# A new order table for a planned attention and gated MLP kernel

## The chip, the core and the metric

The kernel is one program on one core of a Trainium2 chip. What is measured is the time of one execution on the device, in microseconds (us); lower is better. A core has five engines that run their own instruction streams in order: TensorE (PE), VectorE (DVE), ScalarE (ACT), GpSimd (POOL) and SyncE (SP), which here issues nearly all DMA transfers.

## What is computed

```python
scores = (1/sqrt(64)) * q @ k.T                     # 8 batches, 8 heads, 576 positions, head dim 64
cum    = cumsum(log(clip(f, 1e-4, 1)), axis=-1)
scores = where(causal, -1e9, scores + cum[..., :, None] - cum[..., None, :])
attn   = softmax(scores, axis=-1)
x      = (attn @ v), the heads side by side         # 8 x 576 x 512
gate   = sigmoid(causal depthwise conv of x, 5 taps, conv_w)
out    = (gate * (x @ w_val)) @ w_out
```

All is float32 in and out, and the result must keep float32 precision. For that most products are made of two parts: a value is split into a rounded part that PE takes in one pass (type fp32r) and the rest, and three products of parts are added up.

## The kernel before

The work is a list of some three thousand steps. `tile_decay_attention_gated_mlp` first adds every step to a `Plan`, each with the engines that may do it, what it reads and writes, and the PSUM banks that it takes. Then `Plan.order` unpacks the string `ORDER`: a word for each step, which says which step comes next and on which engine it runs, and behind these a word for each set of PSUM banks, which says where it lies. The instructions are issued in that order, and dependencies are added so that each engine and the DMA queue keep it. So the table alone decides three things: the order on every engine, the engine of a step that several may do (`any_`), and the bank of each product (`home`).

```python
        steps, homes = words[:len(self.nodes)], words[len(self.nodes):]
        ...
            self.home[k] = list(range(h, h + self.width[k]))
        for w in steps:
            yield self.nodes[w >> 3]["fn"], codes[w & 7]
```

The heads are taken in 32 pairs, four to a batch. For pair i, buffer i % 2 of most tiles is used (names with two numbers in the trace, one for even and one for odd pairs):

- `load_pair` and `load_rest` load q and k as `Xr` (608 KB) and v as `vt` (576 KB). From the fifth pair on `plan_t` splits `Xr` into `Xh` (a cast) and `Xl` (a subtraction). `Xl` has one buffer for all pairs.
- `plan_s` makes the scores on PE in four groups, which take 4, 2, 2 and 1 banks of the 8: the first two groups hold the longest rows. To each the decay is added by products with `st` and `pkr` or `pl`. DVE adds the mask and takes the row minimum (line 469, `red`), ACT takes the exponential (line 473, `ex`) and writes `P`; then the banks are free. DVE transposes `P` into `T` (line 510).
- `plan_pt` sends `T` to `U` in eight DMA transfers of 196 KB, the "blocks", and the row sums through DRAM (`zd`, then two `zb`).
- `plan_pv` multiplies `U` with `vt` on PE (54 instructions of the program, PV below), DVE scales the result into `x` (line 559), and `x` is split into `xh` and `xl` (line 571, the subtraction). The gate's convolution runs as products on PE for the first four pairs (`CV`), and later as multiplications (`tm`, lines 282 and 284) and additions (line 602, `gate`), and a tanh.
- `plan_moe`, once a batch, makes `val` on PE (Mv: 16 steps of six matmuls of 288 columns), multiplies it by the gate on DVE (line 632, `h`), splits `h` into `hh` and `hl` (line 646), and makes the output (Mo: two steps of six matmuls of 512 columns for each tile of rows), which goes out through `ot`.
- `plan_cw` and `plan_w` decode the weights `conv_w`, `w_val` and `w_out` into `wall` in the first part of the run. They come in pieces of 512 KB, which land in `ot` or `gate`.

All DMA but one goes through SP's queue (line 289).

Of the kernel before, what the change touches and what calls it, by code (L numbers as in the profile page):

```python
# [40 lines left out]
ORDER = (
    "c-n1J2}qRb|DSp1a88|5=hQiMPMuTd)H!udom1zOG=sE+w1TvPbPLi7(hAZF(hAH9(k)20AYFrW6Vf$EHzBPc-GVfOw1od|wY&A>|GqrW^FH6>^Zk53-&X|+"
    "f?j}lAS(z8GJ^1+_aGPOCMW@tf*|1CARZJ8VuJ2~YQWn-J3u?(e}W!@K7k-G3|I<%3`)S8LH9u|pnC9A5CSHHwuAP<w?jKYcfnmCGI$%j7t{}W0H%UDU<FtN"
    "-UZcyaWD<E8LCX7!2-}0C>v&hUW7)W?NBGw0(OA|;0|aETn$yi`=AZr!-zrX3B)LL2s#a2gw8^{p{vkw=n}LUybs<E-hhf>9pF~50@e*Sz;?j;;Jx5Rm>t#%"
    "KLFFDbi#iIKZ3Qv<H$kyGuRPW7km_c7xn};4z{H9!r#DN!N%d&VGm%=lp**c_&n?bYzf>C_Q0m$w_#Uc3D`9FDLf224x0m$fNii<@EO<!m<a#?3b>A1gs;MP"
    "0!wfp<s)nzPDr_pLZ(ntI4QxDy#N~!rHB9>pa9H3EX4)Xq?}55j0gay5lDD_3Kb5(3Gj=E?v$;-9O43kgjhzf;R}c{Kn&Nw`w=UM%PCAm6EKX}lQIbmAT|&$"
    "Q$`SnQ??*G0W*9ir4D%`r4`);OduTawUmP?4am1Cw^B}|%%?yRF`yM_2R2j2Qb0&QJchWJf<^QKlPP;rX~+RUhwKN~NEFhHJeVp%;*kNQ961MkM7fark*&z%"
    "$X}2TQKLu#x+B$qI)enzJ*gPfxl}6p4bqN6qFIPV6az&@T}z!tNl+h<OQ=Uk4w{deMLk2RQLCuW$S267Xfr~NxQlv)tWEm`m;yS{=aDd!4k18yp+$%XsO!i@"
    "z=>D}wjf^O6zCvg1-OE&MhDPZ^lhXC{T5e?-T<8FC>jN6M%N-Pp&QY=5dCNXatr+eO@M&$%jkP(Je~pBm3A|=71e|Y5ohsGOmi9^@;tRAZ8(*OaiAtrXV4?5"
    "N#b(q7<wvoBb9_%Nu5hoVXzo*+8SDl5kgRD^XMq57Bz_upqQA$skpRilo1ocC?E|e3uF^rgE@-QL7b2isWyx#Z9j^ZCQoyvvD0*ENsK>jH_@C{kEu@kiP(XP"  # L50
    "rFk)DQODBI_|CKd<b2vLOb_a}w0;a7e<f`?O@hPVsv$851E<E-L0I^^X=GdrrUTQAX~*z!dmui1H|BcUgESHTCgvby4OfSk<1b-8r^WCM_%~@fd=>t7ngO?o"
    "Gvgm)Jh*235awChQ;Z7_!?i%}V?LxUV(hqXNEp`+>49`YUZuUpjAQyC?=ZuVLCACbA^a$0jJ%BBz&wJi;3GH}=@=1=og{bT+wnd4etZXh7(amDPkaIy!B60)"
    "@t^RuxEf*;4vjrYtj0Cs>WNoz_lf<)bGQ~94%<z9Po9NL5C@19><jW7v4<$Y0t60rfrugK2{P<3af)~hM<(d77Q!;ojP;Q`gwIqrHbxpwe@Cn$NeE#AjK(0W"
    "LKY!+3G0w$h!1;!peFoD7LhiH=Lvj*oJ1o%Ab?3b2`EwodxXFyeIh3ac+wTZcC3zcoUoTrjopR4PN37a5iBH7`WZqUsTnJ#-6phP8%eTsRQfg20n#xnEgheJ"
    "gyc$Rr|Z&BV*TlZBvJY^k~#e>_A{vu8%uvgdPTa4y-R|Td$9oY4e1H#e)^X5VJwFHfHaYgf{tL%lRl6h5(v<#bS14WolKUHyVD!e+tV53E2N(E=JewvHF=fR"
    "k<O*Hr1Qx;8U5*JNV9|)@)BX1K!@&SXlRRs!Sofv1a><OOq?grrFY;q2p_SF>Ako&>7Z14Mk{RycZ|_U`;gv7JI4sn9%Gwm7Fv`xi2I!Gq&>xQGDdOZI73D?"
    "4VLkdmdHR7HRJ{C@eF&$?>K<|2D>ezlZK?zi3c)fac45BnUahTSOU?Lah7%@1DVPpM#)0r&J1;ih3q72iRUu{<Z#9%#xxC+QAHl5?ag4N4$>OP&oZxM^wP#@"
    "rx+L-IpZo#kV;B@l{rgWqz%z_ke6wF3^GkYl&2a}pE3yaCbEUdOzq2{(e0^DVk?<PZzBikqYQLb7g<VQWQ;RDWezfy7^ldN)B}vsjKPfYjG>Gn#wtTaKf;L7"
    "Ut~;W_)=~3X~sI^H2o6!D%nWCOyAA~m|pq}{f~?b^rehO<`{iC3&FfWZ(<&%&(jCV4$2<-Bt4o6$s#a^$hYVx=p3euqF_>)HS~jY3)4ptGKpCp_C30jsiA0@"
    "HL3OV7-c;p#tgIHXILnXtN^o$QlHw&q-51mkd$`jE($<7&HR<A$l6DtQizlb%s`el>nNp_63wd4I!WPDI9at>&*_($-4tQg1oIZNF-u6f!Gva7vU(_M%zI2;"  # L60
    "W)mBmd5!Wk3(Q!i@5@@D&oDQcX3hq^mc5wuk}1ukGEj`06jJ6qb1>^C_EJ`F7Mo$qe9LUjx<k2|)tRNrWM&R!5g89Dqm-_!H<{kdwyejL1b-sSm?>wBX6<Hw"
    "$eg1rP*$_H@kNX~?2RllL&rGEhO(yFN|vADX81BY*;v*ryO-U?jx$EtSJ^rii8an1WdBJy%yMw57$FvuRh8M08Q}P{W0^Iq6RaqwF7q9wiNDCc#Y(b{Wj19Z"
    "sHa)=td7jy%*(8Mtk>+HGTZnz)&&-hx`%ax1#o`ib2vy&g1yT2vOZFT90KQ2&Oz2Xn?^mw=dq|9fVz#X<FKg;&Q{Ko91-;)zm9X3-<`RKBV{e}FL4GkWz=h#"
    "gZzV>C4Mh|h_9jkk~z)4%J1hK=FIX(`4Q?%&Pe7A=LBad=eNvN{ub&j&RfoU&KPH&^O4Wv-s4PVTBuO&B&UvgpS8x3atYb*b2!=5Y!VmCRb&gZf$Y<qO^!Aj"
    "B0y#{xqGOtY!B6veSs6nK1f|)?c`6f=2#;FgrGXxAevx>skPb5taa92zDCfP%@Mq3;n^}Sm`xA}1$L1|fM!z#0fAG{oK0g#1&6Z_QGd=>2-xgrIVZCHTr*eB"
    "7PDXFxVT5DQIU>2oLwub7R+Sp*|pq<f<CG$C(4}`D8ysg^VzckGkYtylln5-n6q85mOYu>z-{J|a$2}=v+r=BIjw@NqRs41!DDU*mzTrL=@qmI8U;_eU4qlu"
    "*qnCmRl$9(H0N@5lVFj%TQn@VkbPZpliI_b;GU=6$Q~5D5ZsoW<MxS$sAJT9qCwFW>NW1DXh>wrnWT1##zn270q(M(OEfK76L5uXB9U-YP?ZzNu?aO|SI%SV"
    "tmKl^B321wIZkn}s43^N&?|gOt<Cu<CnPiqkL4_J4-0PypNhsMr-e!3DtCceBRnDO$XOJ<kbLCs5nd4X<N)F&5lL7tTor+M1Tj*4PzV)v=TOBs-nxh>d_zU?"
    "ewR>q9uY@8kb@PzlzpIz#6dBK7Z$yiT+0#iC{jSG<h_;M6s}5;Qib%FoOKCDs+AI?Lh0_DksKe-BE2ga5l#s;JiL5Z_&^d9gXIqCgs?_@O1vzb6?ThFylN?0"
# [729 lines left out]
```

## Time and profile before

| what | us |
|---|---|
| median of three executions | 564.57 |
| all three | 564.47, 577.34, 564.57 |
| the profiled execution | 569.91 |
| its span, first to last instruction | 568.2 |
| PE busy / DVE / ACT / POOL | 486.0 / 445.7 / 369.9 / 293.0 |

The profile is of one execution. The span runs from its first to its last instruction. "Busy" is the time in which an engine had an instruction in work; a PE that is busy may still run at the lower of its two clocks, which the column of the granted clock tells (1.00 is 2.4 GHz, 0.50 is 1.2 GHz).

### The profile page before, as it was taken

How to read it: one execution, taken by the hardware profiler on the slowest of the kernel's cores; microseconds unless marked ns; L12 is line 12 of the kernel's file. 1: busy time of each engine (PE TensorE's matmuls, PEld its weight loads, DVE VectorE, ACT ScalarE, POOL GpSimd, SP SyncE). 2: the span in 40 equal slices, each digit the busy share in tenths (PEclk: the TensorE clock that was granted, in tenths of full speed). 3: DMA queues.
4: the chain of work that ended last, by engine and by line, in shares of the span. 5: the costliest groups of instructions: out<-in, count | busy, mean ns of one | idle time of the engine just before them, and what ended most of it. 6: DMA issues, size and time to landing. Idle time of an engine off the chain costs nothing.

```text
span 568.2 us, 15877 instructions
## 1 busy us (share of the span) xinstructions
PE 486.0 (86%) x6096; PEld 419.9 (74%) x6096; DVE 445.7 (78%) x1150; ACT 369.9 (65%) x968; POOL 293.0 (52%) x296
## 2 busy tenths in 40 slices
...
GB/s 267 110 216 244 203 226 181 184 172 146 204 223 204 193 215 237 205 206 247 181 258 222 221 174 269 252 190 239 221 240 194 238 278 167 185 207 179 101 39 92
DMA packets 50268, 114.08 MB, mean 201 GB/s; under 512 B 11664, under 2 KB 28048, under 8 KB 50192
## 3 DMA queue, kind: packets, MB, share of 16 engines
...
## 4 chain that ended last, share of the span: by engine, by line
DMA 27%; PE 25%; DVE 19%; ACT 10%; SPq 8%; issue 6%; POOL 5%; DVEq 0%; POOLq 0%; ACTq 0%
PE banks L262 25%; DMA Xr<-in_x_dram 13%; SPq L289 8%; DMA U<-T 8%; DVE T L510 6%; DVE banks L469 5%; ACT P L473 4%; DMA out_dram<-ot 2%; POOL Xl L390 2%; DMA zb<-zd 1%; ACT Xh L277 1%; DVE x L559 1%; DVE gate L602 1%; DMA cwu<-in_conv_w_dram 1%; ACT tm L282 1%
## 5 line engine op out<-in xcount | busy, mean ns | idle before, releaser
L473 ACT ACTIVATE P<-banks,negm 128x192 f32<-128x192 f32 (+3 forms) x256 | 145.9, 578 | 37.2 <-DVE negm L469 35.9
L469 DVE CUSTOM_DVE_ANT_0 banks<-banks,mk 128x192 f32<-128x192 f32 (+3 forms) x256 | 137.8, 579 | 14.8 <-PE banks L262 9.3
L510 DVE STREAM_TRANSPOSE T<-P 128x640 f32<-128x640 f32 (+3 forms) x128 | 120.3, 962 | 21.6 <-ACT P L473 14.9
L262 PE MATMUL banks<-U,vt 64*64 64x128 f32 (+1 forms) x3456 | 112.2, 271 | 28.6 <-DMA U<-T 18.9
L262 PEld LDWEIGHTS banks<-U,vt 64*64 64x64 f32 x3456 | 106.6, 143 | 38.0 <-issue 20.8
L262 PE MATMUL banks<-xh,wall 128*128 128x288 f32 x512 | 113.5, 305 | 7.5 <-ACT P L473 4.5
L602 POOL TENSOR_TENSOR gate<-gate,tm 128x576 f32<-128x576 f32 x64 | 90.9, 1421 | 33.9 <-DVE gate L602 11.3
L390 POOL TENSOR_TENSOR Xl<-Xr,Xh 128x512 fp32r<-128x512 f32 (+1 forms) x56 | 78.3, 1415 | 47.0 <-PE banks L262 20.9
L262 PEld LDWEIGHTS banks<-xh,wall 128*128 128x128 f32 x512 | 85.6, 191 | 14.2 <-ACT P L473 5.9
L262 PE MATMUL banks<-wall,hh 128*128 128x512 f32 x288 | 93.2, 405 | 2.4 <-ACT x L277 1.2
L282 ACT ACTIVATE tm<-x,cw 128x576 f32<-128x576 f32 x101 | 76.5, 775 | 17.9 <-DVE gate L602 12.1
L262 PE MATMUL banks<-xl,wall 128*128 128x288 f32 x256 | 76.2, 298 | 0.0
L262 PE MATMUL banks<-st,pkr 64*128 64x288 f32 (+3 forms) x320 | 52.1, 363 | 25.7 <-ACT P L473 12.8
L262 PEld LDWEIGHTS banks<-wall,hh 128*128 128x128 f32 x288 | 52.2, 190 | 15.0 <-issue 1.7
L262 PEld LDWEIGHTS banks<-st,pkr 64*128 64x128 f32 x320 | 29.9, 191 | 42.7 <-ACT P L473 15.5
L571 POOL TENSOR_TENSOR xl<-x,xh 128x576 fp32r<-128x576 f32 x28 | 40.5, 1446 | 32.3 <-ACT xh L277 19.2
L262 PE MATMUL banks<-wall,hl 128*128 128x512 f32 x144 | 56.6, 393 | 0.0
L473 ACT ACTIVATION_READ_ACCUMULATOR P<-banks,negm 128x1 f32 x256 | 51.0, 199 | 0.0
L262 PEld LDWEIGHTS banks<-xl,wall 128*128 128x128 f32 x256 | 48.9, 191 | 0.3
L602 DVE TENSOR_TENSOR gate<-gate,tm 128x576 f32<-128x576 f32 x48 | 40.7, 848 | 8.3 <-ACT tm L282 7.5
L277 ACT CAST Xh<-Xr 128x512 fp32r<-128x512 f32 (+1 forms) x38 | 23.5, 644 | 32.5 <-DMA Xr<-in_x_dram 32.4
L559 DVE TENSOR_TENSOR x<-banks,zb 128x256 f32<-128x256 f32 x64 | 24.2, 411 | 25.3 <-ACT x L277 24.6
(106 smaller groups left out, 739.1 us busy)
## 6 DMA issues: line engine op xcount, KB each, us to landing
...
Xr<-in_x_dram SPq DMA_DIRECT2D x32, 608.0 KB, 6.8
...
```

What stands on the lines that cost most here:

```text
L262: nc.tensor.matmul(out, lhsT=lhsT, rhs=rhs, start=start, stop=stop)
L277: (eng.copy if eng is nc.scalar else eng.tensor_copy)(out=out, in_=in_)
L282: eng.activation(out=out, in_=in_, func=AF.Copy, scale=col)
L289: lambda e: (nc.sync if e == "SP" else nc.scalar).dma_start(out=out, in_=in_), reads, writes, **kw)
L390: eng.tensor_tensor(out=Xl[r][:, a - XQ:e - XQ], in0=Xr[r][:, a:e], in1=Xh[r][:, a - XQ:e - XQ].bitcast(F32), op=ALU.subtract)
L469: nc.vector.tensor_tensor_reduce(out=sl, in0=sl, in1=add, op0=ALU.add, op1=ALU.min, scale=-0.125, scalar=3.0e38, accum_out=negm[r][:, col])
L473: nc.scalar.activation(out=dst, in_=bank(key)[:, a0:a0 + ext], func=AF.Exp, bias=negm[r][:, col], scale=-1.0, accum_out=zs[r][:, col])
L510: dve("DT", dt(2 * w), base + 0.35 + 0.03 * n, lambda t=t, w=w: nc.vector.transpose(out=blocks(64 * FB[t], [(32, 2), (64, 2 * t + 3), (CW, ...
L559: nc.vector.tensor_tensor(out=bass.AP(to.tensor, to.offset, [to.ap[0], (P, 4), (32, 2), (1, 32)]), in0=bank(keys[n])[:, 0:L0 // 2].rearran ...
L571: any_("xl", {"POOL": 1.4, "DVE": 0.67}, p, lambda eng: eng.tensor_tensor(out=xl[s], in0=xv, in1=xh[s][:, :].bitcast(F32), op=ALU.subtract ...
L602: any_("cva", {"POOL": 1.4, "DVE": 0.67}, pp, lambda eng, to=to: eng.tensor_tensor(out=gt, in0=gt, in1=to, op=ALU.add), [tk, gk], [gk])
```

## The change

Only the string `ORDER` is another one. It holds as many words as before, and the steps, their buffers and their dependencies are the same. The transfers of the blocks were taken as longer when it was made, and the DMA queue as served first come, first served.

```diff
--- before.py
+++ after.py
@@ -39,70 +39,70 @@
 ORDER = (
-    "c-n1J2}qRb|DSp1a88|5=hQiMPMuTd)H!udom1zOG=sE+w1TvPbPLi7(hAZF(hAH9(k)20AYFrW6Vf$EHzBPc-GVfOw1od|wY&A>|GqrW^FH6>^Zk53-&X|+"
...
+    "c-nnZc}SFN`<{7caaNsGXVqDCR-IL6)me2`omFR*^cbWiq!py6Agv&+Agv&+Ag#cxApHu`Q;;5m^dzLmApH{33er=MW{{TfJEyF3zVpZLeR!Ycdair9?)xEu"
...
```

Of the 402 sets of banks 224 lie elsewhere. Of the 32 second score groups, three (of the 4th, 12th and 13th pair) took a bank with no other step of PE between them and the last one that wrote it; now none does. Of the steps that may run on several engines, these changed engine (numbers of instructions, counted in the two programs):

| what | POOL | DVE | ACT |
|---|---|---|---|
| `xl`, line 571 | 28 to 10 | 4 to 22 | |
| `hl`, line 646 | 26 to 8 | 22 to 40 | |
| `gate` additions, line 602 | 64 to 58 | 48 to 54 | |
| `Xl`, line 390 | 56 to 52 | 0 to 4 | |
| `pl` casts, line 277 | 14 to 40 | 26 to 2 | 24 to 22 |
| `Xh` casts, line 277 | 10 to 18 | 8 to 2 | 38 to 36 |
| `hh` casts, line 277 | | 9 to 19 | 39 to 29 |
| `ot` from banks | | 3 to 0 | 33 to 36 |
| `wall` casts and products | 4 to 5 | 11 to 7 | 1 to 4 |

On PE, the place where the second pair's scores end and the third pair's may begin. `Xr_76` is `Xr` of an even pair (here the third), `Xr_77` of an odd one (the second), `U_87,vt_89` are PV of an even pair (here the first). Before:

```order
L262 MATMUL banks<-st,pkr 128x320 x2
L262 MATMUL banks<-st,pkr 128x192 x2
L262 MATMUL banks<-Xr_77 128x320 x2
L262 MATMUL banks<-Xr_77 128x192 x2
L262 MATMUL banks<-U_87,vt_89 64x128 x8
L262 MATMUL banks<-U_87,vt_89 64x64 x2
```

After, at the same place on PE:

```order
L262 MATMUL banks<-st,pkr 128x320 x2
L262 MATMUL banks<-st,pkr 128x192 x2
L262 MATMUL banks<-Xr_77 128x320 x2
L262 MATMUL banks<-Xr_77 128x192 x2
L262 MATMUL banks<-st,pkr 128x288 x4
L262 MATMUL banks<-Xr_76 128x288 x4
L262 MATMUL banks<-st,pkr 128x448 x2
L262 MATMUL banks<-Xr_76 128x448 x2
L262 MATMUL banks<-U_87,vt_89 64x128 x8
```

The first two score groups of the third pair stood behind the whole PV of the first pair, and now stand ahead of it.

On SP, the transfers around the blocks of the fourth pair (`U_88<-T_86` of an odd pair). Before:

```order
L289 DMA Xr_77<-in_x_dram 128x1216
L289 DMA zd_70<-zt_98 128x32
L289 DMA ot<-in_w_out_dram 128x1024
L289 DMA Xr_76<-in_x_dram 128x1216
L289 DMA U_88<-T_86 32x1568 x2
L289 DMA zb_100<-zd_70 64x4x128 x2
L289 DMA U_88<-T_86 32x1568 x3
L289 DMA vt_89<-in_v_dram 128x1152
L289 DMA U_88<-T_86 32x1568 x3
L289 DMA zd_67<-zt_97 128x32
```

After, at the same place on SP:

```order
L289 DMA Xr_77<-in_x_dram 128x1216
L289 DMA ot<-in_w_out_dram 128x1024
L289 DMA vt_89<-in_v_dram 128x1152
L289 DMA zd_70<-zt_98 128x32
L289 DMA U_88<-T_86 32x1568 x8
L289 DMA zb_100<-zd_70 64x4x128 x2
L289 DMA Xr_76<-in_x_dram 128x1216
L289 DMA ot<-in_w_out_dram 128x1024
L289 DMA zd_67<-zt_97 128x32
L289 DMA U_87<-T_85 32x1568 x8
```

The load of `Xr` of the seventh pair (`Xr_76`) went ahead of the blocks, and two `zb` and a load of `vt` stood between them; now the eight follow each other, and that load of `Xr` goes behind them. The loads of `vt` of the fifth pair (`vt_89`) and of a piece of `w_out` now stand ahead of the pair's `zd`.

On PE, the rows ahead of PV of the twelfth pair (`U_88,vt_90`). `Xh_79` is of the fourteenth pair, `wall,hh` and `wall,hl` are Mo. Before:

```order
L262 MATMUL banks<-U_87,vt_89 64x64 x6
L262 MATMUL banks<-st,pl 128x64
L262 MATMUL banks<-Xr_76 128x64
L262 MATMUL banks<-st,pkr 128x288 x4
L262 MATMUL banks<-Xh_79 128x288 x4
L262 MATMUL banks<-Xh_79,Xl_80 128x288 x4
L262 MATMUL banks<-Xl_80,Xh_79 128x288 x4
L262 MATMUL banks<-st,pkr 128x448 x2
L262 MATMUL banks<-Xh_79 128x448 x2
L262 MATMUL banks<-Xh_79,Xl_80 128x448 x2
L262 MATMUL banks<-Xl_80,Xh_79 128x448 x2
L262 MATMUL banks<-U_88,vt_90 64x128 x8
```

After, again up to PV of the twelfth pair on PE:

```order
L262 MATMUL banks<-wall,hl_123 128x512
L262 MATMUL banks<-wall,hh_120 128x512 x2
L262 MATMUL banks<-wall,hl_124 128x512
L262 MATMUL banks<-st,pkr 128x448 x2
L262 MATMUL banks<-Xh_79 128x448 x2
L262 MATMUL banks<-Xh_79,Xl_80 128x448 x2
L262 MATMUL banks<-Xl_80,Xh_79 128x448 x2
L262 MATMUL banks<-st,pkr 128x288 x4
L262 MATMUL banks<-Xh_79 128x288 x4
L262 MATMUL banks<-Xh_79,Xl_80 128x288 x4
L262 MATMUL banks<-Xl_80,Xh_79 128x288 x4
L262 MATMUL banks<-U_88,vt_90 64x128 x8
```

The first row of the piece before is the end of PV of the eleventh pair. After it came the smallest score group of the thirteenth pair, two groups of the fourteenth, and PV of the twelfth. Now the third score group of the thirteenth pair (8 instructions) and four steps of Mo (24 matmuls, of which the last row of `hl_123` and those behind it are shown) stand between as well.

## Rows read from the trace of the kernel before

**Rows 1.** The page: the span, busy times, GB/s in 40 slices.

```profile
span 568.2 us, 15877 instructions
...
PE 486.0 (86%) x6096; PEld 419.9 (74%) x6096; DVE 445.7 (78%) x1150; ACT 369.9 (65%) x968; POOL 293.0 (52%) x296
...
GB/s 267 110 216 244 203 226 181 184 172 146 204 223 204 193 215 237 205 206 247 181 258 222 221 174 269 252 190 239 221 240 194 238 278 167 185 207 179 101 39 92
```

**Rows 2.** Four stretches: busy time and count of each engine, granted clock, DMA share.

```profile
0.00:140.00 140.00, 105.27 (x1165) 86.28 (x1167) 113.86 (x291) 71.05 (x204) 49.01 (x75) 0.84 0.74 196
140.00:280.00 140.00, 119.97 (x1651) 105.34 (x1648) 114.78 (x300) 104.49 (x270) 87.53 (x81) 0.97 0.77 210
280.00:420.00 140.00, 126.58 (x1707) 108.96 (x1705) 118.16 (x310) 108.25 (x287) 91.19 (x84) 0.98 0.84 226
420.00:568.00 148.00, 134.22 (x1578) 119.35 (x1578) 98.87 (x251) 86.15 (x210) 65.28 (x58) 0.98 0.66 174
```

**Rows 3.** Waits of PE in the whole run: us, times, longest.

```profile
PE banks L262 <- ACT P L473: 23.3, 16, 4.8
PE banks L262 <- DMA U<-T: 18.9, 9, 5.0
PE banks L262 <- DVE h L632: 10.8, 10, 3.8
...
PE banks L262 <- DMA zb<-zd: 3.2, 2, 2.6
PE banks L262 <- DMA out_dram<-ot: 2.9, 1, 2.9
```

**Rows 4.** Waits of PE from 28 to 36 us.

```profile
PE banks L262 <- ACT P L473: 4.8, 1, 4.8
PE banks L262 <- DMA U<-T: 4.1, 1, 4.1
```

**Rows 5.** Waits of PE from 76 to 96 us.

```profile
PE banks L262 <- DMA U<-T: 6.2, 2, 5.0
```

**Rows 6.** Waits of PE from 210 to 230 us.

```profile
PE banks L262 <- DMA U<-T: 5.0, 2, 3.2
```

**Rows 7.** Waits of PE from 120 to 215 us.

```profile
PE banks L262 <- DVE h L632: 6.6, 4, 3.8
```

**Rows 8.** Two stretches of 20 us, columns as in the second group.

```profile
80.00:100.00 20.00, 13.21 (x156) 10.70 (x156) 11.51 (x28) 5.12 (x19) 7.82 (x8) 0.83 0.81 202
...
220.00:240.00 20.00, 15.68 (x169) 13.80 (x167) 9.93 (x23) 10.40 (x27) 8.34 (x7) 0.83 0.88 231
```

**Rows 9.** DMA issues from 219 to 237 us: KB each, median us to landing.

```profile
Xr<-in_x_dram SPq DMA_DIRECT2D x1, 608.0 KB, 9.1
...
zd<-zt SPq DMA_DIRECT2D x1, 16.0 KB, 8.8
```

**Rows 10.** Groups by form: busy us, mean ns of one | idle before.

```profile
L602 DVE TENSOR_TENSOR gate<-gate,tm 128x576 f32<-128x576 f32 x48 | 40.7, 848 | 8.3 <-ACT tm L282 7.5 <-POOL gate L602 0.2
L571 POOL TENSOR_TENSOR xl<-x,xh 128x576 fp32r<-128x576 f32 x28 | 40.5, 1446 | 32.3 <-ACT xh L277 19.2 <-DVE xh L277 10.2 <-DVE zr L479 2.6
...
L277 DVE CAST pl<-pk 64x64 fp32r<-64x64 f32 x26 | 15.8, 608 | 0.2
...
L571 DVE TENSOR_TENSOR xl<-x,xh 128x576 fp32r<-128x576 f32 x4 | 3.5, 876 | 1.5 <-ACT xh L277 1.5
```

**Rows 11.** One tile, pl: ns of one, shortest, median and longest.

```profile
L277 DVE CAST pl<-pk x26: 178/312/1358, 45.4 to 478.8; 64x64 fp32r<-64x64 f32 x26
...
L277 POOL CAST pl<-pk x14: 230/234/351, 7.3 to 412.6; 64x64 fp32r<-64x64 f32 x14
```

**Rows 12.** One line, 602: ns of one, shortest, median and longest.

```profile
L602 DVE TENSOR_TENSOR gate<-gate,tm x48: 709/758/1790, 143.9 to 544.4; 128x576 f32<-128x576 f32 x48
```

**Rows 13.** The chain that ended last: shares by engine.

```profile
DMA 27%; PE 25%; DVE 19%; ACT 10%; SPq 8%; issue 6%; POOL 5%; DVEq 0%; POOLq 0%; ACTq 0%
```

**Rows 14.** The chain in order of time, last PE run: start, us, count.

```profile
547.45 17.08 PE banks L262 x84
```

More of the change, by code (lines that the diff above doesn't have):

```diff
@@ L46 @@
[L46 to L69, printed above, removed]
@@ new lines @@
+    "_JE)u7l;R9g5;ne=q0EIj0Gh?R*)2A1nmUzp!MLppbwy3a0vJh5E%9ugaJPQCE(jZ&7dcs7SJ=06nYEv2-FVR2S>nmKs!PAz+E6RSO(n=?*;XP9)hW04p;#e"
+    "fp<f-U>r;XZHFpTXfO-31ImU4pqHRdXfrelwSZmV0JsGj16M<p@IGh*_y}SYx(Gdqn1&8QXQAEDA?PY}2|5mK2k(bBgFC=t*aox}tblcc4X~ZCKKM0oFSrqA"
+    "hjqf=!u|u+q_o1H!@A&c<RJVp>?5oVJ_`51hTyMZmXu!jJ=i$>DeMN!nKBNZh9_WQ*hAO_*dq8Dd>VWJb_ccuo&%GB?XXqw3D{NG1{e$+g`t5}_zlz|oC&PM"
+    "fs`dUA!QeUOrfT5QqICeDR)qp5P_6f%ITDv6gD6N_5s}~3IK}G0Z$Ml#4y4PtfkbaU=jU@5yb5j7r;aeAZAiN!R8RJQlh|S$}(aBaU~@H+)tT6tRTixegfuG"
@@ new lines @@
+    "j-+fL_NKf`X#%z(&md^<7WB=OIwS~*f{y_Jya7poPo{JN9JmJF1?){dnIb}p;RjPtNICK%f`-H+b;wr0jC3K{$VtEqZ$<`?4tP7ziaeOw3!Fgyf*b()0TyBu"
+    ">4%?18c;FB9DqSFP<GTWKu78qBpG!%bqaWle1sAq_^9)#&yhNW1O-EVLQSLOh_^^H!il(^`V_f{x`5n<m_@xt0_YpaB~%bWK;J{DQAqSEii-Y-Jch1CbfRn1"
+    "t|FI#-H0yqB5((}0z5=<&>MgNje;~G00;r%Kn2jRaMfrAB#Ks`Yta_;JDe8XigKbG(U;MDNHh9K>aEmjQ~=eFevukQ4X4(k8c-)wZ=+wLA$UCg7-}MQB=u+1"
+    "a_W8bRO&{m5VDL`Kth<g)RolTX*HM*)GVHaNn*~Sz-i5C7RVY}2Wd&G$2cK83@VL@QDFiQ8wQuQiS9x5W1tu*rW!JacBRqrx-=tZ2JKIyrJ2)0L{XX-!%mAq"
```

94 lines of the change are left out of this document (55 added, 39 removed).

## The prediction

> **What bounds the kernel now.** The page comes first: PE is busy for 486.0 of 568.2 us, DVE for 445.7 [rows 1]. A share over the whole run hides stages, so four stretches come next [rows 2]. In the first 140 us PE is busy for 105.3 us at a mean granted clock of 0.84, while DVE works 113.9 us: there the weights are decoded, and PE waits. From 140 to 280 us PE idles 20.0 us, from 280 to 420 us 13.4 us, and in the last 148 us 13.8 us. So PE leads from the second stretch on, with DVE second (114.8 and 118.2 us of 140), and POOL has room everywhere. What an order can take out is mainly PE's idle time, 82 us, and time at the lower clock.
>
> Then the list of PE's waits [rows 3]. The largest entry is ACT's exponential, which frees score banks: 23.3 us. The second is the landing of the blocks in `U`: nine waits, 18.9 us. Then come the multiplication by the gate (`h`), which frees an Mv bank, 10.8 us, and two other landings, 3.2 and 2.9 us. The block waits are few and long: the same list for three windows finds 4.1 us ahead of the first PV [rows 4], 6.2 us in two waits ahead of the fourth [rows 5], and 5.0 us in two ahead of the twelfth [rows 6]. These make 15.3 of the 18.9 us.
>
> Last, the queue. The `zd` transfer of 16 KB that follows an `Xr` load of 608 KB takes 8.8 us to land, the load itself 9.1 us [rows 9]. So a small transfer here waits for the big one ahead of it; a load in front of blocks delays them. By "DMA: Bandwidth & Descriptors" of the Trainium skill, section "Queues, rings and completion order", completion is not first in, first out per issuing engine. Read as freedom from the queue, that would leave the block waits where they are (rival D); the pair of rows goes against it, since the small one landed behind the big one.
>
> **The change, part by part.** All sums are against the profiled execution, 569.91 us, which is 1.7 us longer than its span.
>
> 1. *First PV.* Two score groups of the third pair now go ahead of it, so PE has work during the 4.1 us. Whether they can start depends on banks: just before, PE stood 4.8 us for the exponentials that free them [rows 4]. Ends: 0 and -4.1 us. I take half, -2.
>
> 2. *Fourth PV.* The blocks now follow each other, with the seventh `Xr` load behind them instead of ahead, and neither `vt` nor `zb` between. By the queue's rows a load of this size in front costs a small transfer several us. The 6.2 us [rows 5] should go for the most part; but PE now has another order there too, and PV comes after slightly less score work. Ends -6.2 and -2; I take -5.
>
> 3. *Twelfth PV.* Four Mo steps, 24 matmuls, and a score group now stand between it and the eleventh. The last run of PE in the chain does 84 matmuls in 17.08 us [rows 14], 0.203 us each, and most of its matmuls are Mo: 24 make 4.9 us, as long as the wait of 5.0 us [rows 6]. It costs nothing, since that Mo work has to be done anyway. Ends -5.0 and -3; I take -5.
>
> 4. *Banks behind `h`.* Of the 10.8 us, 6.6 lie between 120 and 215 us [rows 7], around score groups that follow Mv. The three second score groups that took a bank with no step between are gone. But DVE, which runs `h`, gets more to do. Ends -8 and +3; I take -4.
>
> 5. *Other landings*: 18.9 - 15.3 = 3.6 us of blocks and 3.2 + 2.9 us of `zb` and `ot` [rows 3]. The loads were moved all along the queue, and nothing in the rows says in which places it helps. Ends -9 and +3; I take -3.
>
> 6. *Clock.* The two stretches with the waits of parts 2 and 3 had a granted clock of 0.83 [rows 8], so some 6.8 of 20 us each at 1.2 GHz; run at 2.4 GHz that work would take 3.4 us less, in both 6.8 us. If the waits go, I expect that more than half of this goes too. Ends -6.8 and 0; I take -4.
>
> 7. *The start.* SP now issues a 512 KB piece of `w_val` ahead of the first `Xr`. At the 267 GB/s of the first slice [rows 1] that is 2.0 us later for the first scores, in part hidden by the table of decays that is made meanwhile; the decoding starts earlier. Ends 0 and +2; I take +1.
>
> 8. *DVE.* By means of the kernel before [rows 10]: 18 more `xl` x 0.876 = 15.8 us; 18 more `hl` instructions, which make 11 whole tiles, also x 0.876 = 9.6; 6 additions x 0.848 = 5.1; 24 fewer `pl` casts x 0.608 = -14.6. The rest (10 `hh`, 4 `Xl`, 2 others more; 6 `Xh`, 3 `ot`, 4 `wall`, 3 small ones fewer) comes to within 2 us of nothing. The sum is about +16 us of DVE work. DVE makes 19% of the chain that ended last [rows 13], so the price on the path is 16 x 0.19 = 3 us. The cover is DVE's own idle time, 122.5 us in the span, 21.8 of 140 in the third stretch. If that cover were gone, the price would be up to 16 us. If faster `xl` and `hl` (0.876 against POOL's 1.446 us) shorten chains, it is below nothing, -3. I take +3, nearest the chain's share.
>
> 9. *POOL* loses 18 x 1.446 = 26.0 us for `xl` and a like sum for `hl` and additions, and gains 26 casts and 8 `Xh`. It was busy for half of the span; this is worth nothing directly.
>
> 10. *Waits that the new order brings.* Every fixed order has places where a transfer or a bank comes later than meant; the old one has 35.8 us of such waits in [rows 3] without the exponentials. ACT's 23.3 us I leave as they are. For new ones of the first kind, ends 0 and +15; I take +5, a seventh of the old sum, since PE has more steps between a pair's last of the three large score groups and its PV in 21 of the 32 pairs, and fewer in 8 (counted in the two orders).
>
> Sum: -2 - 5 - 5 - 4 - 3 - 4 + 1 + 3 + 5 = -14 us, so 556 us on the scale of the profiled execution. The median of the three runs is 564.57, 0.991 of that execution, so the prediction is 551 us, 2.4% faster. A difference of about 2% is what a measurement of this kernel tells from no change; 2% is 11.3 us, 553.3 us.
>
> **The rivals.**
>
> *A: the waits only move.* PE's waits for blocks fall but those for ACT and DVE grow by the same. For it: the exponentials already are the largest wait, and they hang on DVE's reductions, which get 16 us of company. Against it: PE's idle time is three times as dense in the first stretch as in the third, where the same steps run with the same engines, so the density is not a law of this work. Time: 564 us, give or take 5.
>
> *B: DVE becomes the bound from 140 to 420 us.* There it is busy for 233 of 280 us [rows 2], 83%. The mechanism is one lock: a `pl` cast on DVE takes 178 ns at best and 1358 at worst, 312 in the median, while POOL's takes 230 to 351 [rows 11]; a `gate` addition on DVE takes 709 to 1790 [rows 12]. The long ones are about one POOL instruction longer. The subtractions that come to DVE have two inputs in SBUF like those additions. Were each of some 40 of them held by half of a POOL instruction, 0.7 us, that is 28 us more, 44 us in all, of which two thirds would lie here: 233 + 29 = 262 us, 94%. Before, DVE gave 113.9 + 114.8 us in 280 us [rows 2], 82%, under decoding. At 85% 262 us take 308 us, 28 more than now; with 15 us of the gains above kept, the run gets 13 us longer, 577 us. It decides from about 240 us of DVE work there. Against it: the mean of the `gate` additions is only 0.09 us above their median (848 against 758), so most are not held; and the `pl` casts, which are held most, leave DVE. By "SBUF — State Buffer" of the Trainium skill, section "SBUF: two separate sides", the shared pair of ports is a lock for a whole instruction, also against DVE instructions with two SBUF inputs; the range of the additions agrees that it happens, their median that it is rare. Taken for every moved instruction, the rule gives this rival.
>
> *C: more goes than I counted.* Most of the 35.8 us of waits without the exponentials vanish, and with them the slow clock in the opening: -30 us, 535 to 540 us. For it: the long waits came with head-of-line loads, and these moved everywhere. Against it: the waits are spread over several releasers [rows 3], and DVE is as loaded in the opening as before.
>
> *D: the queue isn't served in order,* so the order's assumption doesn't hold, and block waits stay: about 566 us. The rows on the queue speak against it.
>
> **How the numbers follow.** The forecast, 543 to 559 us, has 0.52, of which two thirds (0.34) lie under 553.3. A has 0.20, B 0.09, C 0.16, D 0.03. Faster by over 2%: 0.34 + 0.16 = 0.50. Slower by over 2%: B, 0.09, and 0.01 of A's upper end, 0.10. Within 2%: the rest, 0.40. The range takes in the forecast, the upper part of C from 537 us, and A up to its upper end of 569 us; outside lie half of C and all of B, some 0.17.
>
> **What would show it.** In the new profile PE's waits for `U` should be under 8 us in all, with none over 3 us ahead of the fourth and twelfth PV; the first two stretches should hold less PE idle time by 10 us together; the clock of the stretches that now show 0.83 should be over 0.9; DVE should be busy for 455 to 465 us with PE's waits for `h` no longer than 10.8 us. If DVE is over 90% busy between 140 and 420 us and PE waits mainly for DVE and the exponentials, B is right. If PE's idle time is 80 us again, with other entries on top, A is.

## The result, and the profile after

| | before | changed |
|---|---|---|
| median, us (four runs each, in turn on one chip) | 569.70 | 537.10 |
| lowest and highest, us | 564.47, 577.34 | 534.20, 544.62 |
| the profiled execution, us | 569.91 | 539.46 |
| its span, us | 568.2 | 537.7 |

The ratio is 0.949, with a 95% interval of 0.939 to 0.958. It leaves out two of the four runs before and one of the four after, which are over 1.5% longer than the fastest of their kernel, and so it isn't the quotient of the two medians. The forecast was 551 us, and 543 to 559 its own band. The time lies below that band and just inside the lower end of the wide range, 537 us, which was set there for rival C. On the span the change saves 30.5 us, where the sum had 14.

The page of the changed kernel, its span and busy times (for [rows 1]):

```profile
span 537.7 us, 15860 instructions
...
PE 474.2 (88%) x6096; PEld 411.7 (77%) x6096; DVE 457.4 (85%) x1169; ACT 369.3 (69%) x963; POOL 247.3 (46%) x282
```

PE's idle time falls from 568.2 - 486.0 = 82.2 to 537.7 - 474.2 = 63.5 us, which is 18.7 us. The other 11.8 us are busy time: the same 6096 matmuls (as the trace counts them) are in work for a shorter time.

The four stretches of the changed kernel (for [rows 2], same columns: PE, PEld, DVE, ACT, POOL, then granted clock, DMA share, GB/s):

```profile
0.00:140.00 140.00, 102.22 (x1174) 83.99 (x1175) 115.64 (x308) 79.25 (x223) 51.63 (x84) 0.90 0.78 212
140.00:280.00 140.00, 131.16 (x1826) 115.24 (x1825) 122.37 (x315) 113.85 (x296) 85.22 (x79) 0.97 0.86 223
280.00:420.00 140.00, 133.02 (x1866) 116.92 (x1866) 130.68 (x327) 113.75 (x302) 81.78 (x88) 1.00 0.88 242
420.00:538.00 118.00, 107.79 (x1238) 95.56 (x1234) 88.73 (x222) 62.48 (x146) 28.67 (x32) 0.98 0.61 164
```

The counts in brackets are the progress. By 140 us PE has started 1174 matmuls, and 1165 before: for PE the opening gave next to nothing. In each of the next two stretches it does some 160 to 175 more than before. PE, DVE and the DMA engines are all fuller there: from 280 to 420 us 95%, 93% and 88%, against 90%, 84% and 84%.

PE's waits in the whole run of the changed kernel (for [rows 3]):

```profile
PE banks L262 <- ACT P L473: 26.3, 22, 5.4
PE banks L262 <- ACT x L277: 9.0, 4, 5.0
PE banks L262 <- ACT Pl L473: 6.8, 5, 3.1
PE banks L262 <- DMA U<-T: 5.9, 2, 3.4
...
PE banks L262 <- DVE Xl L390: 2.5, 1, 2.5
PE banks L262 <- DVE h L632: 2.2, 2, 1.2
...
PE banks L262 <- DVE x L559: 1.4, 2, 1.0
```

Blocks fall from 18.9 to 5.9 us, `h` from 10.8 to 2.2, and `zb` and `out` are gone. New is a wait for ACT's `x` (a cast for the convolution), 9.0 us. Where these lie shows in the same list for the time from 140 us on, first of the kernel before:

```profile
PE banks L262 <- ACT P L473: 8.9, 8, 1.8
PE banks L262 <- DMA U<-T: 8.6, 6, 3.2
PE banks L262 <- DVE h L632: 6.9, 9, 1.4
PE banks L262 <- DVE x L559: 5.8, 6, 2.4
...
PE banks L262 <- DMA zb<-zd: 3.2, 2, 2.6
PE banks L262 <- DMA out_dram<-ot: 2.9, 1, 2.9
```

and of the changed one, from 140 us on:

```profile
PE banks L262 <- ACT P L473: 12.1, 11, 2.4
PE banks L262 <- DMA U<-T: 3.4, 1, 3.4
PE banks L262 <- ACT Pl L473: 2.7, 3, 1.4
PE banks L262 <- ACT x L277: 1.4, 1, 1.4
PE banks L262 <- DVE h L632: 1.0, 1, 1.0
...
PE banks L262 <- DVE x L559: 0.3, 1, 0.3
```

From there on the waits for DVE (`h` and `x`) shrink from 12.7 to 1.3 us and those for transfers (`U`, `zb`, `out`) from 14.7 to 3.4; those for the exponentials grow by 3.2. In the first 140 us the block waits shrink too, from 10.3 to 2.5 us, but waits for ACT's `x` (7.6 us), for `Pl` (3.6 more) and for `Xl` (2.5) take their place.

DVE has a list of waits of its own. Before, its first row was

```profile
DVE x L559 <- ACT x L277: 24.6, 12, 7.4
```

and in the list of groups by form of the changed kernel line 559 has 7.7 us of idle time ahead of it, of which 2.0 us are this wait:

```profile
L559 DVE TENSOR_TENSOR x<-banks,zb 128x256 f32<-128x256 f32 x64 | 24.3, 413 | 7.7 <-PE banks L262 4.6 <-ACT x L277 2.0 <-DMA U<-T 0.8
```

While DVE stands at `x`, all that is queued behind it stands too: mask additions, transposes for the next blocks, `h`. The prediction had nothing on this row.

### The profile page after: what moved, and what is told of

Same layout as the page of the kernel before. It is cut to its first block, busy times and chain, and to the rows that moved or that the text cites. A ratio compares the mean times of both kernels' runs of the same rounds, so it can differ in the third digit from the quotient of the medians.

```text
span 537.7 us, 15860 instructions
## 1 busy us (share of the span) xinstructions
PE 474.2 (88%) x6096; PEld 411.7 (77%) x6096; DVE 457.4 (85%) x1169; ACT 369.3 (69%) x963; POOL 247.3 (46%) x282
## 4 chain that ended last, share of the span: by engine, by line
PE 32%; DVE 22%; DMA 21%; ACT 12%; SPq 6%; issue 5%; POOL 1%; DVEq 0%; POOLq 0%; ACTq 0%
PE banks L262 31%; DMA Xr<-in_x_dram 10%; ACT P L473 7%; DVE banks L469 6%; SPq L289 6%; DVE T L510 4%; DMA U<-T 3%; DMA gate<-in_w_val_dram 2%; DVE gate L602 2%; DMA vt<-in_v_dram 2%; DVE x L559 2%; DMA zb<-zd 2%; DMA ot<-in_w_out_dram 1%; DVE negm L469 1%; ACT tm L282 1%
## 5 line engine op out<-in xcount | busy, mean ns | idle before, releaser
L473 ACT ACTIVATE P<-banks,negm 128x320 f32<-128x320 f32 (+3 forms) x256 | 145.7, 577 | 38.9 <-DVE negm L469 34.1
L469 DVE CUSTOM_DVE_ANT_0 banks<-banks,mk 128x320 f32<-128x320 f32 (+3 forms) x256 | 138.0, 579 | 12.3 <-PE banks L262 6.6
L510 DVE STREAM_TRANSPOSE T<-P 128x1152 f32<-128x1152 f32 (+3 forms) x128 | 119.9, 958 | 14.1 <-ACT P L473 10.5
L262 PEld LDWEIGHTS banks<-U,vt 64*64 64x64 f32 x3456 | 97.9, 137 | 15.8 <-issue 8.7
L262 PE MATMUL banks<-U,vt 64*64 64x128 f32 (+1 forms) x3456 | 102.1, 262 | 8.7 <-DMA U<-T 5.9
L390 POOL TENSOR_TENSOR Xl<-Xr,Xh 128x576 fp32r<-128x576 f32 (+1 forms) x52 | 73.1, 1420 | 64.8 <-PE banks L262 32.2
L602 POOL TENSOR_TENSOR gate<-gate,tm 128x576 f32<-128x576 f32 x58 | 82.9, 1429 | 17.3 <-ACT tm L282 7.6
L262 PEld LDWEIGHTS banks<-wall,hh 128*128 128x128 f32 x288 | 51.8, 189 | 14.7 <-ACT P L473 2.0
L602 DVE TENSOR_TENSOR gate<-gate,tm 128x576 f32<-128x576 f32 x54 | 45.6, 848 | 3.0 <-ACT tm L282 1.9
L492 POOL TENSOR_SCALAR Pl<-Pl,zr 128x64 f32<-128x64 f32 x32 | 20.4, 637 | 50.8 <-DVE zr L483 45.3
L469 DVE DVE_READ_ACCUMULATOR2_ANT negm<- 128x1 f32 x288 | 40.1, 139 | 0.0
L262 PE MATMUL banks<-Xh,Xl 64*128 64x288 f32 (+1 forms) x280 | 36.1, 307 | 2.5 <-DVE Xl L390 2.5
```

What stands on the lines that cost most here:

```text
L262: nc.tensor.matmul(out, lhsT=lhsT, rhs=rhs, start=start, stop=stop)
L390: eng.tensor_tensor(out=Xl[r][:, a - XQ:e - XQ], in0=Xr[r][:, a:e], in1=Xh[r][:, a - XQ:e - XQ].bitcast(F32), op=ALU.subtract)
L469: nc.vector.tensor_tensor_reduce(out=sl, in0=sl, in1=add, op0=ALU.add, op1=ALU.min, scale=-0.125, scalar=3.0e38, accum_out=negm[r][:, col])
L473: nc.scalar.activation(out=dst, in_=bank(key)[:, a0:a0 + ext], func=AF.Exp, bias=negm[r][:, col], scale=-1.0, accum_out=zs[r][:, col])
L492: pool("Pn", 0.25, p + 0.02, lambda: nc.gpsimd.tensor_scalar(out=Pl[r], in0=Pl[r], scalar1=zr[r][:, 8:9], scalar2=0.0, op0=ALU.mult, op1=A ...
L510: dve("DT", dt(2 * w), base + 0.35 + 0.03 * n, lambda t=t, w=w: nc.vector.transpose(out=blocks(64 * FB[t], [(32, 2), (64, 2 * t + 3), (CW, ...
```

## The experiments

Twelve kernels were run, each made from one of the two by another `ORDER` alone, so that all compute the same. Where a step could not stay in its place without blocking another, it was moved as little as would do. Ratios are to the kernel before, with 95% intervals. The theories: that PV's distance from its blocks carries the gain (W); that the engine choices do (E); that the queue's order does; that PV and what follows it on the other engines must be moved together (J); and that only the whole plan fits, order, engines, banks and queue (K).

**1 and 2, engines.** Experiment 1 is the changed order with DVE's, ACT's and POOL's steps on the engines of before (PE and SP the same); experiment 2 is the order of before with the changed engines. A row of the first on POOL:

```diff
+L571 TENSOR_TENSOR xl_109<-x_101,xh_103 128x576
+L479 TENSOR_SCALAR zr_95<-zs_93 128x9
+L492 TENSOR_SCALAR Pl_84<-Pl_84,zr_95 128x64
```

> The changed table, but every step of ACT, DVE and POOL that changed engine is back on its engine of before, at its new place in the order; PE and SP as in the changed kernel. Theory W (PE no longer stands at PV for blocks, since the order puts more work in between): the profiled run stays near 540 us (535 to 548), ratio to the kernel before 0.94 to 0.96, PE's idle time before the PV matmuls under 12 us. Rival E (the steps moved from POOL to DVE shorten chains and that is the gain): 555 to 570 us, ratio over 0.975.

Measured: 568.24 us, 1.002 (0.997 to 1.007). The whole gain is gone, with only 2.3 us of block waits left on PE. PE's waits:

```profile
PE banks L262 <- ACT P L473: 32.2, 22, 5.7
PE banks L262 <- ACT Pl L473: 10.4, 3, 4.6
PE banks L262 <- ACT x L277: 8.9, 7, 4.2
PE banks L262 <- POOL Xl L390: 5.9, 7, 2.4
```

> The table of before, with the engines of the changed one for the steps of ACT, DVE and POOL; PE and SP as before. Theory W: 560 to 575 us, ratio 0.99 to 1.02, idle time before PV matmuls still about 28 us (22 to 33). Rival E: 540 to 550 us, ratio under 0.97.

Measured: 577.47 us, 1.011 (1.003 to 1.019). So the engines alone give nothing (the interval even lies just above 1), and the order without them gives nothing. Experiment 1 also shows that block waits are not a currency: they are gone and the time is that of before.

**3 and 4, PV's distance.** Experiment 3 is the kernel before with PV later on PE: in 25 pairs one to four more steps stand between a pair's scores and its PV, counted in the two orders. Experiment 4 is the changed kernel with PV earlier. The other engines and the banks are untouched. The first piece of experiment 3 on PE (two score groups of the third pair go ahead of the first PV, as in the change):

```diff
+L262 MATMUL banks<-st,pkr 128x448 x2
+L262 MATMUL banks<-Xr_76 128x448 x2
+L262 MATMUL banks<-st,pkr 128x288 x4
+L262 MATMUL banks<-Xr_76 128x288 x4
 L262 MATMUL banks<-U_87,vt_89 64x128 x8
```

> The table of before, with nothing changed but the place of PV on PE: in 25 of 32 pairs it goes 1 to 6 steps later, so that in all 594 in place of 549 steps stand between a pair's scores and its PV (the changed kernel has 595). Theory W in its narrow form (the distance on PE is the cause): PE's idle time before the PV matmuls falls from 28.6 to under 14 us, and the run is 10 to 20 us faster, ratio 0.965 to 0.98. Rival M (one place alone is no cure, DVE then stands at the multiplication behind PV, and the waits move): ratio 0.985 to 1.015, with DVE's wait in line 559 over 30 us where it was 25.3.

Measured: 628.89 us, 1.104 (1.095 to 1.112). Its waits, first of PE and then of DVE:

```profile
PE banks L262 <- ACT P L473: 63.2, 33, 6.1
PE banks L262 <- DVE h L632: 18.8, 15, 3.6
...
PE banks L262 <- DMA U<-T: 5.6, 2, 4.4
```

```profile
DVE x L559 <- ACT x L277: 63.6, 15, 7.3
```

The block waits fall to 5.6 us, as in the changed kernel, and DVE stands at `x` for 63.6 us: PV is later, `x` is not, and what is queued behind `x` on DVE gets late, then the exponentials that wait for it.

> The changed table, with PV on PE moved up 1 to 4 steps where the kernel before had less in between (549 is the aim, some can't move). Theory W in its narrow form: the wait for blocks comes back, idle time before the PV matmuls 15 us or more in place of 8.7, 545 to 555 us, ratio 0.965 to 0.98. Rival M: the wait for blocks stays under 12 us, since the blocks themselves are issued earlier in the changed order, and the ratio stays 0.94 to 0.96.

Measured: 607.59 us, 1.066 (1.058 to 1.073), with block waits of 8.6 us on PE and DVE waiting 75.5 us for PE's banks. W has fallen: moving PV alone costs in either direction. M's waits came in both runs, its times in neither.

**5 and 6, `x` together with PV, and alone.** Experiment 5 moves PV, `x`, `xh` and `xl` later as one; experiment 6 moves `x` and its parts one to five steps later on DVE and ACT (PE nearly the same). A piece of experiment 6 on DVE:

```diff
-L559 TENSOR_TENSOR x_102<-banks,zb_100 128x4x64 x2
 L693 SCALAR_TENSOR_TENSOR gate<-gate 128x512
 L695 TENSOR_SCALAR ot<-ot 128x512
 L469 ISA banks,negm_92<-banks,mk 128x320
 L469 ISA negm_92 128x1
+L559 TENSOR_TENSOR x_102<-banks,zb_100 128x4x64 x2
```

> The table of before with PV and what follows it at once (the scaling in line 559, its small copy, the split of x) moved later on all engines together: PV has 592 steps of PE in front of it in all where it had 549, in 27 pairs more, and DVE and ACT come to the scaling as much later. Theory J (DVE and ACT stand in line behind a late PV, so its place must fit on all three engines): the wait for blocks falls as in the run with PV alone late, under 9 us, DVE's wait in line 559 stays under 25 us, and the run is 12 to 25 us faster than before, ratio 0.955 to 0.98. Rival K (no single distance is the cause, the gain is spread over the whole plan): 560 to 585 us, ratio 0.985 to 1.03.

Measured: 694.13 us, 1.217 (1.209 to 1.225). Both waits that J named behaved: the list has no wait of PE for blocks, and DVE's stand at `x` is 19.3 us. The time went elsewhere, first of all to PE's waits for `x` and for the exponentials:

```profile
PE banks L262 <- DVE x L559: 52.6, 31, 4.3
PE banks L262 <- ACT P L473: 50.6, 27, 5.0
```

> The table of before with only the scaling of x, its small copy and its cast moved 1 to 5 steps later on DVE and ACT; PE but for a few places, POOL and SP as before. Theory J: DVE's wait in line 559 falls from 25.3 to under 15 us, what stood behind it (mask and minimum) comes earlier, and the run gains 3 to 12 us, ratio 0.98 to 0.995. Rival K: within 1% of before, since x then is late for its own readers.

Measured: 593.37 us, 1.040 (1.034 to 1.047). DVE's stand at `x` falls to 6.0 us, as wished, and PE waits 23.9 us for `x` instead of 8:

```profile
PE banks L262 <- ACT P L473: 24.8, 18, 5.8
PE banks L262 <- DVE x L559: 23.9, 21, 2.1
PE banks L262 <- DMA U<-T: 17.0, 6, 5.3
```

`x` frees the banks of PV, so a later `x` holds PE up. The long row of DVE before is no prize that can be taken by itself, and J has fallen with it. K's times (560 to 585 us, and within 1%) failed as well: both runs are slower than any theory had them.

**7 and 8, the queue alone.** Experiment 7 is the changed kernel with SP's order of before, experiment 8 the reverse; all other engines are untouched. A row of experiment 8 is the piece on SP shown with the change.

> The changed table with the transfers of SP in the order of before (as near as the dependencies allow); PE, DVE, ACT and POOL as in the changed kernel. If the queue's order carries the gain: 555 to 570 us, with PE's wait for blocks back over 15 us. Theory J (the queue's order must fit the engines' too): slower than the changed kernel by 2 to 6%, ratio 0.96 to 1.01. Rival: the queue's order hardly matters, ratio 0.94 to 0.96.

Measured: 588.57 us, 1.027 (1.019 to 1.036), longer than any of the three had it. PE's block waits are back at 19.0 us in the profiled execution, which with 591.46 us is the longest of its four.

> The table of before with SP's transfers in the order of the changed one; the engines as before. If the queue's order carries the gain: 540 to 555 us, wait for blocks under 10 us. Theory J: no gain, ratio 0.99 to 1.04. Rival: hardly any difference, ratio 0.99 to 1.01.

Measured: 597.46 us, 1.045 (1.038 to 1.052), block waits 18.1 us; only J's upper end comes near. The new queue order needs the new order on the engines, and the other way round.

**9, loads between blocks.** The changed kernel with 49 loads of `Xr` and `vt` between a pair's fourth and fifth block instead of ahead of them. A piece on SP:

```diff
-L289 DMA Xr_76<-in_x_dram 128x1216
 L289 DMA ot<-in_w_out_dram 128x1024
 L289 DMA zd_67<-zt_97 128x32
-L289 DMA U_87<-T_85 32x1568 x8
+L289 DMA U_87<-T_85 32x1568 x4
+L289 DMA Xr_76<-in_x_dram 128x1216
+L289 DMA U_87<-T_85 32x1568 x4
```

> The changed kernel, with 49 loads of Xr and vt (pairs 4 to 30) moved from ahead of a pair's blocks to between its fourth and fifth block on the same queue; nothing else. If the queue serves transfers in the order of issue and the place of the loads is a part of the gain, the fifth and later blocks land behind a load of 590 or 608 KB: U waits on PE of 15 us or more (5.9 now) and 545 to 575 us. If the queue lets 64-partition blocks pass a load, or if blocks have slack everywhere by now, U waits stay under 8 us and the time is 535 to 541 us.

Measured: 730.06 us, 1.285 (1.276 to 1.293). Both expectations fail: PE waits 1.9 us for blocks, and yet this is a third slower than the changed kernel. Its longest waits of all engines:

```profile
ACT Xh L277 <- DMA Xr<-in_x_dram: 148.7, 18, 11.5
POOL Xh L277 <- DMA Xr<-in_x_dram: 90.4, 9, 12.8
```

and its stretch from 280 to 420 us, columns as above:

```profile
280.00:420.00 140.00, 95.99 (x1149) 83.22 (x1147) 77.37 (x199) 67.97 (x183) 51.90 (x51) 0.80 0.58 144
```

SP issues in order, so a load behind four blocks is not issued before all that stands ahead of it may go: the pair's row sums (`zt`, sent as `zd`), output pieces (`ot`) and the transposes. SP's own waits:

```profile
SPq L289 <- DVE zt L484: 123.0, 20, 12.9
SPq L289 <- ACT ot L673: 121.6, 23, 11.7
SPq L289 <- DVE T L515: 75.3, 30, 5.6
```

In the changed kernel the same three are 37.1, 42.5 and 40.3 us. The DMA engines idle meanwhile (0.58 busy, 0.88 in the changed kernel), `Xr` lands late, and ACT and POOL stand at `Xh`. That ACT's work queued behind `Xh` then holds up the row sums and outputs that the next load stands behind, and so closes a loop, is the reading of these rows and has no run of its own.

The question that the run was made for is answered by its issue and landing times. A block issued right behind a load takes 7.9 us to land in the median (28 blocks), the other 228 take 4.9, and each of the 28 lands 0.3 to 1.1 us after the load. All 464 transfers on SP's queue land in the order of their issue, here and in the traces of all other kernels. So a load in front does hold a block up, by some 3 us; but here the place at which the loads are issued cost far more.

**10, the start.** The changed kernel with the first `Xr` and `vt` ahead of the piece of `w_val`:

```diff
+L289 DMA Xr_76<-in_x_dram 128x1216
+L289 DMA vt_89<-in_v_dram 128x1152
 L289 DMA ot<-in_w_val_dram 128x1024
-L289 DMA Xr_76<-in_x_dram 128x1216
-L289 DMA vt_89<-in_v_dram 128x1152
```

> The changed kernel with the first Xr and vt ahead of the 512 KB piece of w_val on the queue, as they were before the change; nothing else. If the opening is paid for by that piece (step 7 of the prediction, some 1 us), the time is 535 to 538 us and PE starts its first scores earlier by 1 to 2 us. If the opening is bound by other work by then, no difference within the interval. If the w_val piece is waited for itself, 540 us or more.

Measured: 531.66 us, 0.934 (0.927 to 0.942), the fastest of all, though its interval touches that of the changed kernel. Its first stretch:

```profile
0.00:140.00 140.00, 104.70 (x1211) 85.62 (x1213) 119.75 (x315) 81.34 (x225) 52.54 (x85) 0.90 0.81 217
```

That is 37 matmuls more by 140 us. The first `Xr` lands at 6.2 us where the changed kernel has 8.2, and PE's first scores start at 7.1 us and not at 8.3, as expected. Whether this is the gain isn't shown. The fifth pair's `Xr` load (start, us) lands 3.0 us earlier than in the changed kernel, at 56.1 and not 59.2 us:

```profile
48.19 10.96 DMA Xr<-in_x_dram
```

```profile
45.76 10.38 DMA Xr<-in_x_dram
```

But in experiment 11, which keeps the piece of `w_val` in front, it lands earlier still, at 55.2 us, and PE has started 1245 matmuls by 140 us:

```profile
46.22 9.00 DMA Xr<-in_x_dram
```

```profile
0.00:140.00 140.00, 107.02 (x1245) 88.45 (x1249) 120.21 (x318) 81.55 (x227) 51.86 (x84) 0.89 0.81 218
```

So one execution of nearly the same opening differs from the next by more than the edit was thought to bring.

**11, more work for DVE.** The changed kernel with 29 of POOL's 58 additions to `gate` on DVE:

```diff
-L602 POOL TENSOR_TENSOR gate<-gate,tm 128x576
+L602 DVE TENSOR_TENSOR gate<-gate,tm 128x576
```

> The changed kernel with 29 of the 58 additions to gate that POOL makes given to VectorE, spread over the run: about 29 x 0.85 = 25 us more DVE work, on 457. If VectorE's time is by now the bound from 140 us on (93% busy at 280 to 420), the time rises by 60 to 100% of that: 552 to 562 us, with PE's waits for DVE longer by 10 us or more. If its idle time takes the work up (step 8's price, a fifth of it), 540 to 544 us. If POOL was the late one at gate, 530 to 537.

Measured: 543.32 us, 0.954 (0.948 to 0.960), no difference from the changed kernel that the intervals show. By the two ratios it is some 3 us longer, which is what step 8's price gives; VectorE as the bound (552 to 562 us) is excluded.

```profile
PE 476.7 (89%) x6096; PEld 412.8 (77%) x6096; DVE 471.4 (88%) x1198; ACT 371.9 (69%) x963; POOL 207.3 (39%) x253
```

DVE is busy 14.0 us longer. That the two profiled spans are the same 537.7 us does not make this free: that execution is the shortest of experiment 11's four, and the changed kernel's is one of the longer of its own. It also was 71 matmuls ahead by 140 us, before nearly all of the moved additions, and has lost that lead by the end; at the changed kernel's 4922 matmuls in the 397.7 us from there on, these are some 6 us, an estimate. So 14 us more work may have cost some 3 to 6 us; the intervals allow nothing, too. The additions took 66.6 us where they had taken 45.6, but other DVE groups got shorter: the `hl` subtractions of 576 columns have a mean of 765 ns against 886, with POOL busy for 40 us less; that POOL is the reason is not shown by itself.

**12, PE's order alone.** The kernel before with PE's order and banks of the changed one; the other engines stay as near to their own order as those banks allow. Still 81 of DVE's 804 steps, 77 of ACT's 655 and 21 of SP's 464 stand elsewhere, so it is not one clean move; nor is experiment 5, with 89 of DVE's, 101 of ACT's and 31 of POOL's 264 (counted in the tables).

> The kernel before with TensorE's order and its choice of PSUM banks of the changed one, the other engines in nearly the order of before (moved only where they would block). If TensorE's order is what carries the gain, 537 to 552 us. If the orders of all engines must fit one another, 570 us or more, with PE waiting over 60 us for ACT's P, DVE's x and the U blocks together (53 us before for ACT P, U and h).

Measured: 794.28 us, 1.396 (1.388 to 1.403), PE's wait for the exponentials 101.6 us.

Several of these runs side by side, each with the same 6096 matmuls, tell one more thing of PE's busy time:

| kernel | span, us | PE idle, us | PE busy, us | mean granted clock |
|---|---|---|---|---|
| experiment 10 | 530.6 | 58.4 | 472.2 | 0.968 |
| changed | 537.7 | 63.5 | 474.2 | 0.962 |
| experiment 1 | 563.1 | 79.8 | 483.3 | 0.958 |
| before | 568.2 | 82.2 | 486.0 | 0.943 |
| experiment 6 | 592.0 | 96.9 | 495.1 | 0.930 |
| experiment 3 | 624.0 | 121.9 | 502.1 | 0.921 |
| experiment 5 | 693.5 | 156.8 | 536.7 | 0.877 |
| experiment 9 | 728.0 | 206.4 | 521.6 | 0.840 |
| experiment 12 | 790.0 | 230.0 | 560.0 | 0.844 |

From the changed kernel to experiment 3, 58.4 us more idle time go with 27.9 us more busy time. To experiment 5 they are 93.3 and 62.5, to experiment 9 142.9 and 47.4. So PE is busy longer where it waits more, at a lower clock; but what one us of waiting brings with it, 0.3 to 0.7 us, depends on the run.

## Why the prediction was right in direction and half in size

The ledger of PE, in us:

| | taken | measured |
|---|---|---|
| steps 1 to 3 and the blocks of 5 (`U`) | -12 and a part of -3 | 18.9 to 5.9: -13.0 |
| step 4 (`h`) | -4 | 10.8 to 2.2: -8.6 |
| step 5, `zb` and `out` | the rest of -3 | 6.1 to 0: -6.1 |
| not in the sum: `x` | 0 | 8.0 to 1.4: -6.6 |
| step 10, new waits | +5 | ACT `x` 7.8, `Xl` 2.5, three small ones 2.8: +13.1 |
| exponentials, left as they were | 0 | `P` 3.0 and `Pl` 2.7: +5.7 |
| small waits that went | 0 | some -3 |
| steps 7 and 8 | +4 | not waits of PE; see below |
| step 6, busy time | -4 | -11.8 |

- **Steps 1 to 3, the blocks: right for their own waits.** The first PV waits 2.5 us for its blocks (4.1 before), near the step's -2; but the exponentials ahead of it cost 11.4 us in the first 40 us where they cost 8.3, and it starts at 38.6 us and not at 34.3. The fourth and the twelfth wait not at all; the list from 200 to 240 us has only 1.7 us of waits in all, and 220 to 240 us shows a granted clock of 1.00. From 76 to 96 us PE now waits 2.5 us for `Xl` and 1.9 for the exponentials, and the clock from 80 to 100 us stays at 0.85.
- **Step 4: right, mis-sized.** The term took -4 and measured -8.6, beyond its end of -8. DVE's larger share did not come in its way.
- **Step 5: right, mis-sized,** -3 against -6.1 for `zb` and `out` and next to nothing for the remaining blocks (3.6 to 3.4 us).
- **Step 6 is the term that failed most.** It priced the clock in two stretches of 20 us alone, at -4, and for these two it was about right: one rose from 0.83 to 1.00, the other hardly moved. PE's busy time fell by 11.8 us over the whole run. By the clock records of the two traces PE was busy at the lower clock for 46.2 us before and for 29.7 us after; at twice the clock 16.5 us of such work take 8.3 less, an estimate. The other 3.5 us are open. Most of the clock's gain lies in the first 140 us, where the granted clock rose from 0.84 to 0.90 although PE idled 3 us longer there than before (37.8 and 34.7 us). So the clock did not simply follow the waits that left.
- **Step 7: mechanism right, price not shown.** The first `Xr` lands 2.0 us later, as worked out. Experiment 10 takes that back and is 7.1 us shorter between the two profiled spans, but its interval touches the changed kernel's, and experiment 11 has the better opening without it.
- **Step 8: work right, price neither shown nor refuted.** It foresaw 16 us more of DVE work and 11.7 came, at a price of +3. Experiment 11 adds 14.0 us more; by the ratios that cost some 3 us, and no difference clear of the noise. DVE's idle time in the changed kernel is still 80.3 us, so the case without cover, 16 us, did not come.
- **Step 9:** POOL's busy time fell by 45.7 us; no run shows what that alone is worth.
- **Step 10 was too low:** +5 against +13.1, inside its end of +15. The exponentials, which it left as they were, took 5.7 more. By the entries that grew, 15.6 us of these 18.8 lie in the opening; there they outweigh what steps 1, 2, 4 and 5 gave up to 140 us, and PE has hardly more matmuls done by then than before.
- **The stand at `x`**: DVE's own list of waits shows it, and the sum has no term for it. It fell from 24.6 to 2.0 us of waiting for ACT, and the wait of PE for `x` from 8.0 to 1.4 us. Experiment 6 shows that the one cannot be had by moving `x` alone.

**The signs, and luck.** PE's waits for `U` (5.9 us), for `h` (2.2) and DVE's busy time (457.4) came as foretold. The idle time of the first two stretches fell by 8.1 us and not 10, and the clock from 80 to 100 us stayed at 0.85. The sum of -14 us is less than half of the 30.5 that came: the time is inside the wide range by 0.1 us, because the range took in a part of rival C, and not because the forecast's own sum came out.

**The rivals.** A is refuted for the run as a whole (PE's idle time falls by 18.7 us) and holds for PE in the opening (the idle time that was set against A is 2.6 times as dense in the first stretch as in the third, and not three times). B's ceiling of 85% is wrong: DVE ran 253 of 280 us from 140 to 420 us, 90%, in a faster kernel, and 262 us of them in experiment 11, 94%, with no loss clear of the noise. So B's own sign came, without its time. The rule that it drew on, from "SBUF — State Buffer" of the Trainium skill, section "SBUF: two separate sides", is not refuted by this: the shorter `hl` of experiment 11 agree with a lock that costs on the order of 0.1 us an instruction (the mean of the `xl` on DVE lies 0.25 us above their median, 1.014 against 0.760 us). B's error was the 0.7 us for each. C had the size, and much of its mechanism: of the 35.8 us of waits without the exponentials that it wanted gone, 27.7 went, and the clock of the opening rose from 0.84 to 0.90. But in the opening other waits came instead, and PE's progress was made from 140 us on. D is refuted for this kernel's queue: in every trace the transfers land in the order of issue, and a block behind a load lands after it (experiment 9).

**What carries the gain.** The prediction added up places. The runs contradict that picture: each part by itself (engines, queue, PV's place, `x`'s place, PE's order with its banks) brings nothing or loses 1 to 40%, and taking the engines or the queue back out of the changed kernel loses all of the gain or more. What is shown is that none of these parts carries the gain alone. That the whole plan does, as K has it in general, is what is left over; K's own times failed, and a rival stands beside it that no run tests: a move in a plan that is fitted as tightly as these may cost something wherever it is made, so that the losses say little of the part that was moved. Engines that run in order pass a delay on to all that is queued behind, and experiments 3, 6 and 9 show this with their rows. Which smallest set of moves would give the 30 us stays open, and so does what the banks are worth, which no run changed by themselves. So does whether the longer transfer times or the queue assumed in order made this plan the better one, since no plan with only one of the two was tried.
